# One PSUM tile of eight banks in place of four tiles of two, in a linear-attention and SwiGLU kernel

## The chip, the cores and the metric

The program runs on one core of a Trainium2 chip. The metric is device time in microseconds (us) of one execution. Three runs of the kernel before gave 236.96, 237.26 and 239.74 us; the median is 237.26 us.

## The reference, cut to what matters

Four batches of eight heads, 768 time steps, 48 features per head. `r`, `k`, `v` and `w` have the shape (4, 8, 768, 48). Step by step a 48 x 48 state per head decays and takes in the outer product of `k` and `v`:

```
y[t]  = r[t] @ (state + (u * k[t]) outer v[t])
state = w[t][:, None] * state + k[t] outer v[t]
```

The eight heads of a time step, side by side, are one row `x` of 384 values (3072 rows in all). Each row then goes through an RMS norm and a gated feed-forward layer of width 1536:

```
xn  = x / sqrt(mean(x*x) + 1e-6) * rms_g
out = (silu(xn @ w_gate) * (xn @ w_val)) @ w_out
```

## The kernel before, in words

The recurrence is cut into 6 chunks of 128 time steps (index m), and each chunk is done for the 4 batches (index j). Within a chunk the recurrence is written as matrix products: `cs` multiplies the logarithms of the decays by two triangular masks to get running sums, `exp` takes their exponential in place in PSUM, `rk` scales r and k by it, `tr` (or the DMA `trd`) turns them, `q` multiplies r by k, `qm` masks the product, `y` multiplies it by v and adds the part of the state, `st`, `sn1` and `sn` make the next state. Then come `xa` (adds the `u` term), `sq`, `rs`, `xn` (the norm), `xt` and `xe` (or the DMA `xd`; they turn the rows), and the feed-forward layer in twelve pieces per chunk: `gv` (gate or value product, 24 per chunk, each of twelve matmuls of 128 columns or of fewer and wider ones), `si` (ScalarE: silu of the gate product, PSUM to SBUF), `hm` (VectorE: value product in PSUM times that), `o` (output product in three parts of four matmuls) and `oo` (copy out of PSUM, then a DMA `od`). `warm` is a matmul of a mask with itself into bank 0; nothing reads what it writes. There are 60 of them.

The order of the work is written out by hand in the string `PLAN` (line 94): one word per step, for instance `si.5.0.11@0`, with the step's name, its indices, the slot of the ring that it writes (`@0`), and an engine where there is a choice (`/A` ScalarE, `/V` VectorE, `/G` GpSimd). For the steps that write PSUM (`dk cs tr q y xt st warm gv o`) the number behind `@` is the PSUM bank, 0 to 7; the reader of a product uses the bank that its writer was given. `cs` and `q` take two adjacent banks and always start at an even one. The steps are emitted in this order (line 537), each engine runs its own in this order, and the schedule is not changed by the framework. The kernel contains no semaphores of its own: the framework works out, from the tiles that each instruction reads or writes, which instruction has to wait for which, and adds the waits.

PSUM has 8 banks of 512 fp32 values per partition. The kernel before declares four tiles of two banks each (line 206), so banks 0 and 1 are tile `ps0`, 2 and 3 `ps1`, 4 and 5 `ps2`, 6 and 7 `ps3`. The profile prints all of them as `ps`. Two helpers hand out views: `b1` one bank, `b2` a whole tile. Every PSUM access of the kernel goes through one of them. Of the plan's words, 714 touch PSUM.

Four places of the plan that the prediction uses (lines 135, 189 to 193, cut):

```
... cs.2.1@6 sn1.2.0 warm.44 st.2.2@3 exp.2.1 sn.2.0 ...
... gv.5.0.5.g@6 gv.5.0.11.g@5 si.5.0.5@1 ...
... hm.5.0.10 gv.5.0.5.v@4 hm.5.0.3 oo.4.1@2/A o.4.0.2
si.5.0.11@0 od.4.1 hm.5.0.5 o.5.0.0@2 ... o.5.1.0@6 ...
... o.5.3.0@7 ... o.5.1.2 od.5.0 o.5.3.2 oo.5.1@0/V od.5.1
oo.5.3@1/A od.5.3
```

The product for `sn.2.0` and `sn1.2.0` was put in bank 1 (`st.2.0@1`), and `hm.5.0.3` reads bank 7 (`gv.5.0.3.v@7`).

Of the kernel before, what the change touches and what calls it, by code (L numbers as in the profile page):

```python
# [9 lines left out]
FP32 = mybir.dt.float32  # L10
# [186 lines left out]
class Env:  # L197


    def __init__(self, ctx, tc, args):  # L200
        self.slot = {}
        self.nc = nc = tc.nc
        self.r, self.k, self.v, self.w, u, self.wgate, self.wval, self.wout, g, self.out = args
        const = ctx.enter_context(tc.tile_pool(name="const", bufs=1))
        ps = ctx.enter_context(tc.tile_pool(name="ps", bufs=1, space=bass.MemoryType.PSUM))
        self.banks = [ps.tile([128, 2, 512], FP32, name=f"ps{i}") for i in range(4)]

        self.u, self.g = u, g

        def ring(name, shape, dt):  # L210
            return const.tile([128, RINGS[name]] + shape, dt, name=name)

        self.in_w = const.tile([128, 2, SB, H, D], FP32, name="in_w")
        self.in_rk = const.tile([128, 2, SB, 2, H, D], FP32, name="in_rk")
        self.in_v = const.tile([128, 2, SB, H, D], FP32, name="in_v")
        self.lw = ring("lw", [SB, H, PD], BF16)
        self.rkA = ring("rkA", [2, H, PD], BF16)
        self.rkT = ring("rkT", [2 * NP, 128], BF16)
        self.qts = ring("qts", [2, NP, 128], BF16)
        self.vb = ring("vb", [SB, H, D], BF16)  # L220
        self.ruk = ring("ruk", [H, D], FP32)
        self.ydr = ring("ydr", [H, D], FP32)
        self.xb = ring("xb", [DM], BF16)
        self.xnr = ring("xnr", [DM], BF16)
        self.xnt = ring("xnt", [KC, TS], BF16)
        self.ht = ring("ht", [FC, TS], BF16)
        self.sg = ring("sg", [TS], BF16)
        self.obr = ring("obr", [DM], FP32)
        self.u_bc = const.tile([128, H, D], FP32, name="u_bc")
        self.st = const.tile([128, 2, SB, NP, 2 * D], BF16, name="st")  # L230
        self.wg = const.tile([128, KC, DF], BF16, name="wg")
        self.wv = const.tile([128, KC, DF], BF16, name="wv")
        self.wo = const.tile([128, FC, DM], BF16, name="wo")
        self.junk = const.tile([128, DM], BF16, name="junk")
        WS = DF // NWG
        n_ht = FC * TS // (2 * KC * WS)
        self.n_ht = n_ht
        self.stage_x = const.tile([128, NSTAGE - n_ht, KC, WS], FP32, name="stage_x") if NSTAGE > n_ht else None

        self.ident = const.tile([128, 128], BF16, name="ident")  # L240
        self.mask_lt = const.tile([128, 128], BF16, name="mask_lt")
        self.mask_nle = const.tile([128, 128], BF16, name="mask_nle")
        self.wcr = ring("wcr", [SB, NP], FP32)
        self.diag = const.tile([128, NSB * SB, H, 1], FP32, name="diag")
        self.rstd = const.tile([128, NSB * SB, 2], FP32, name="rstd")
        self.g_col = const.tile([128, KC], FP32, name="g_col")
        self.ones = const.tile([128, 1], BF16, name="ones")
        self.mhalf = const.tile([128, 1], FP32, name="mhalf")
        lwf = self.lw.rearrange("p a b h d -> p (a b h) d")
        nc.vector.memset(lwf[:, :, D:PD], 0.0)  # L250
        for t, op, fill in ((self.mask_lt, ALU.is_ge, 1.0), (self.mask_nle, ALU.is_gt, -1.0)):
            nc.gpsimd.memset(t, 0.0)
            nc.gpsimd.affine_select(out=t, in_=t, compare_op=op, fill=fill, base=0, pattern=[[-1, 128]],  # L253
                                    channel_multiplier=1)
        nc.vector.memset(self.ones, 1.0)
        nc.vector.memset(self.mhalf, -0.5)
        nc.vector.memset(self.rkA.rearrange("p a b h d -> p (a b h) d")[:, :, D:PD], 0.0)
        make_identity(nc, self.ident)
        nc.vector.memset(self.st, 0.0)
# [11 lines left out]
        getattr(self, fn)(*args, *([ENGINES[eng]] if eng else []))  # L271

    def b2(self, key):
        return self.banks[self.slot[key] // 2]

    def b1(self, key):
        i = self.slot[key]
        return self.banks[i // 2][:, i % 2]

    def pair(self, t, q):  # L280
        return t[:, 2 * q:2 * q + 2, :].rearrange("p a b -> p (a b)")
# [287 lines left out]
```

## Time and profile before

| what | value |
|---|---|
| time of the profiled execution | 236.92 us |
| its span, first to last instruction on the core | 234.7 us |
| median of three runs | 237.26 us |
| TensorE (PE) busy | 206.8 us, 88% of the span |
| VectorE (DVE) busy | 163.4 us, 70% |
| ScalarE (ACT) busy | 123.3 us, 53% |
| GpSimd (POOL) busy | 99.5 us, 42% |
| granted TensorE clock, mean over the span | 0.985 of full speed |

How to read it: an engine is busy while at least one of its instructions is under way, so the shares of engines that work side by side add up to more than the span. A matmul is counted from its start to the modelled arrival of its last result. The granted clock is 1.0 at 2.4 GHz and 0.5 at 1.2 GHz. In the views by time, a line merges neighbouring instructions of one engine, line and shape; the time in brackets is how long the engine had been idle before, with the instruction that ended that idle time.

### The profile page before, as it was taken

To read this page: it belongs to the slowest core of one execution; us is meant where nothing else is said; L and a number is where in the kernel's file an instruction comes from. 1 tells how busy PE (TensorE), PEld (TensorE's weight loads), DVE (VectorE), ACT (ScalarE), POOL (GpSimd) and SP (SyncE) were. 2 spreads that over 40 slices of the span, in tenths; PEclk is the share of its full clock that TensorE was granted. 3 is DMA by queue.
4 is the path that set the end of the run, shared out by engine and by line. 5 is a ranking of instruction groups with operands and counts; after the bars stand their busy time and mean duration, and the time that the engine had idled before them with its cause. 6 is when DMAs were issued, how large, how long until landed. Compare 5 with 4: busy or idle time off the path is not lost.

```text
span 234.7 us, 4827 instructions
## 1 busy us (share of the span) xinstructions
PE 206.8 (88%) x1833; PEld 124.0 (53%) x1844; DVE 163.4 (70%) x275; ACT 123.3 (53%) x213; POOL 99.5 (42%) x143
## 2 busy tenths in 40 slices
PE   7756878999989999998798999899999889999993
PEld 2323567975667657755354455454454434544451
DVE  4668969457998879896977868888675846325331
ACT  3338786474475673678364376554774514135300
POOL 2478876913365662767214698852100200100000
PEclk9997799999999999999999999999999999999999
DMA  7999899997989989986999989931047030200013
GB/s 145 192 237 288 244 309 220 203 220 177 199 183 214 182 172 193 202 172 159 203 190 198 195 154 207 230 98 31 18 90 162 17 87 18 62 22 3 13 63 126
DMA packets 133799, 35.77 MB, mean 152 GB/s; under 512 B 124432, under 2 KB 133776, under 8 KB 133776
## 3 DMA queue, kind: packets, MB, share of 16 engines
q1 hardware_dynamic: 132192, 34.29, 67.1%
q0 software_dynamic: 1584, 1.18, 3.7%
q8 instruction: 14, 0.23, 0.4%
q14 instruction: 9, 0.07, 0.1%
HBM read 26.15 MB, written 4.72 MB: 132 GB/s over the span
## 4 chain that ended last, share of the span: by engine, by line
PE 56%; DVE 20%; ACT 8%; issue 5%; SPq 5%; DMA 4%; DVEq 0%; ACTq 0%
PE ps L493 28%; PE ps L509 18%; DVE ht L501 7%; ACT sg L497 5%; SPq L288 4%; DVE st L423 3%; DVE rkA L364 2%; DVE qts L392 2%; PE ps L356 2%; PE ps L480 2%; DMA in_rk<-in_k_dram 2%; DVE xb L449 2%; DVE xnr L462 1%; PE ps L405 1%; DMA xnt<-xnr 1%
## 5 line engine op out<-in xcount | busy, mean ns | idle before, releaser
L497 ACT ACTIVATE sg<-ps 128x512 bf16<-128x512 f32 x72 | 42.3, 596 | 56.5 <-PE ps L493 32.2
L501 DVE TENSOR_TENSOR ht<-ps,sg 128x512 bf16<-128x512 f32 x72 | 48.0, 687 | 26.3 <-ACT sg L497 17.6
L493 PE MATMUL ps<-xnt,wg 128*128 128x128 bf16 (+2 forms) x356 | 56.3, 296 | 5.4 <-ACT sg L497 1.1
L493 PE MATMUL ps<-xnt,wv 128*128 128x128 bf16 (+2 forms) x353 | 54.4, 292 | 3.1 <-ACT sg L497 1.5
L509 PE MATMUL ps<-wo,ht 128*128 128x384 bf16 x288 | 52.0, 326 | 2.2 <-DVE ht L501 1.1
L493 PEld LDWEIGHTS <-wg 128*128 128x128 bf16 x360 | 28.7, 99 | 21.7 <-issue 6.7
L493 PEld LDWEIGHTS <-wv 128*128 128x128 bf16 x360 | 28.6, 97 | 20.3 <-issue 4.0
L509 PEld LDWEIGHTS <-ht 128*128 128x128 bf16 x288 | 27.5, 98 | 22.5 <-issue 3.8
L445 POOL TENSOR_TENSOR ydr<-in_v,diag 128x384 f32<-128x384 f32 x24 | 20.7, 866 | 28.0 <-DVE diag L440 23.1
L433 POOL TENSOR_TENSOR ruk<-in_rk 128x384 f32<-128x384 f32 x24 | 23.9, 997 | 16.3 <-DMA in_rk<-in_k_dram 10.1
L364 DVE TENSOR_TENSOR rkA<-in_rk,ps 128x768 bf16<-128x768 f32 x24 | 22.4, 950 | 11.8 <-ACT ps L361 10.2
L392 DVE TENSOR_TENSOR qts<-ps,mask_lt 128x1024 bf16<-128x1024 f32 x24 | 29.0, 1219 | 1.9 <-PE ps L389 1.6
L458 POOL TENSOR_SCALAR rstd<-rstd 128x1 f32<-128x1 f32 x24 | 4.6, 190 | 48.4 <-ACT junk L453 47.7
L437 POOL TENSOR_TENSOR ruk<-ruk,u_bc 128x384 f32<-128x384 f32 x24 | 24.0, 1000 | 2.5 <-DMA u_bc<-in_u_dram 1.2
L361 ACT ACTIVATE ps<-ps 128x768 f32<-128x768 f32 x24 | 18.7, 795 | 10.5 <-PE ps L356 10.2
L480 PE MATMUL ps<-mask_lt 128*128 128x512 bf16 x60 | 20.3, 439 | 2.9 <-POOL mask_lt L253 1.4
L423 DVE TENSOR_TENSOR st<-ps,wcr 48x192 bf16<-48x192 f32 x40 | 13.8, 353 | 6.6 <-PE ps L493 2.7
L453 ACT ACTIVATE junk<-xb 128x384 bf16<-128x384 bf16 x24 | 12.5, 519 | 9.8 <-DVE xb L449 9.8
L449 DVE TENSOR_TENSOR xb<-ps,ydr 128x384 bf16<-128x384 f32 x24 | 13.2, 552 | 5.5 <-PE ps L405 3.3
L331 DVE COPY obr<-ps 128x384 f32<-128x384 f32 x14 | 7.8, 556 | 11.9 <-PE ps L509 10.7
L322 ACT ACT_TABLE_LOAD x12 | 15.4, 1283 | 0.9 <-PEq L553 0.7
L459 POOL TENSOR_TENSOR rstd<-rstd,mhalf 128x1 f32<-128x1 f32 x24 | 14.0, 581 | 2.0
(58 smaller groups left out, 201.1 us busy)
## 6 DMA issues: line engine op xcount, KB each, us to landing
in_w<-in_w_dram SPq DMA_DIRECT2D x24, 192.0 KB, 4.2
in_v<-in_v_dram SPq DMA_DIRECT2D x24, 192.0 KB, 3.7
in_rk<-in_r_dram SPq DMA_DIRECT2D x24, 192.0 KB, 3.8
in_rk<-in_k_dram SPq DMA_DIRECT2D x24, 192.0 KB, 3.8
out_dram<-obr SPq DMA_DIRECT2D x24, 192.0 KB, 2.1
ht<-in_moe_w_gate_dram SPq DMA_DIRECT2D x6, 384.0 KB, 5.1
stage_x<-in_moe_w_val_dram SPq DMA_DIRECT2D x4, 384.0 KB, 6.1
wo<-in_moe_w_out_dram POOLq DMA_DIRECT2D x3, 384.0 KB, 5.8
```

The source lines that it names most:

```text
L361: self.nc.scalar.activation(out=ps, in_=ps, func=AF.Exp)
L364: self.nc.vector.tensor_tensor(out=self.rkA[:, self.slot["rkA", m, j], :, :, 0:D], in0=self.in_rk[:, self.slot["in_rk", m], j], in1=self.b ...
L392: self.nc.vector.tensor_tensor(out=self.qts[:, self.slot["qts", m, j]].rearrange("p a q t -> p (a q) t"), in0=self.b2(("qb", m, j)).rearra ...
L423: self.nc.vector.tensor_tensor(out=new[p, :, c], in0=ps[p, :, c], in1=wc[p, :].to_broadcast([D, NP, D]), op=ALU.mult)
L433: self.nc.gpsimd.tensor_tensor(out=self.ruk[:, self.slot["ruk", m, j]], in0=rk[:, 0], in1=rk[:, 1], op=ALU.mult)
L437: self.nc.gpsimd.tensor_tensor(out=t, in0=t, in1=self.u_bc, op=ALU.mult)
L445: self.nc.gpsimd.tensor_tensor(out=self.ydr[:, self.slot["ydr", m, j]], in0=self.in_v[:, self.slot["in_v", m], j], in1=self.diag[:, m * SB ...
L480: self.nc.tensor.matmul(self.b1(("warmb",)), lhsT=self.mask_lt, rhs=bc_mid(self.mask_lt, 4), start=True, stop=True)
L493: self.nc.tensor.matmul(ps[:, a * n:(a + 1) * n], lhsT=w[:, c, f * 128:(f + 1) * 128], rhs=x[:, c], start=(a == 0 and c == 0), stop=(a == ...
L497: self.nc.scalar.activation(out=self.sg[:, self.slot["sg", m, g, i]], in_=self.b1(("gvb", m, g, i, "g")), func=AF.Silu)
L501: self.nc.vector.tensor_tensor(out=self.ht[:, self.slot["ht", m], fs[0]:fs[-1] + 1, t0:t0 + n], in0=self.b1(("gvb", m, g, i, "v")).rearran ...
L509: self.nc.tensor.matmul(ps, lhsT=self.ht[:, self.slot["ht", m], f, j * L:(j + 1) * L], rhs=self.wo[:, f, :], start=(f == 0), stop=(f == FC ...
```

## The change

All of PSUM is declared as one tile of eight banks. `b1` and `b2` return views of the same banks as before (`b2` is called with even numbers only). No step, slot, shape or order changes.

```diff
-        self.banks = [ps.tile([128, 2, 512], FP32, name=f"ps{i}") for i in range(4)]
+        self.banks = ps.tile([128, 8, 512], FP32, name="ps")
...
     def b2(self, key):
-        return self.banks[self.slot[key] // 2]
+        i = self.slot[key]
+        return self.banks[:, i:i + 2]
 
     def b1(self, key):
-        i = self.slot[key]
-        return self.banks[i // 2][:, i % 2]
+        return self.banks[:, self.slot[key]]
```

## Rows read from the trace of the kernel before

**Rows 1.** The page: span, and busy time of each engine with its share.

```profile
span 234.7 us, 4827 instructions
PE 206.8 (88%) x1833; PEld 124.0 (53%) x1844; DVE 163.4 (70%) x275; ACT 123.3 (53%) x213; POOL 99.5 (42%) x143
```

**Rows 2.** The page: shares of the chain that ended last, by engine.

```profile
PE 56%; DVE 20%; ACT 8%; issue 5%; SPq 5%; DMA 4%; DVEq 0%; ACTq 0%
```

**Rows 3.** By time, chunk 2: start us, us, engine, line, operation [idle before, releaser].

```profile
85.19 0.35 DVE L423 TENSOR_TENSOR st<-ps,wcr 48x192 bf16<-48x192 f32 x1
85.45 0.80 ACT L361 ACTIVATE ps<-ps 128x768 f32<-128x768 f32 x1
85.60 0.38 PE L480 MATMUL ps<-mask_lt 128*128 128x512 bf16 x1 [0.19 <-DVE st L423]
...
86.01 0.36 DVE L423 TENSOR_TENSOR st<-ps,wcr 48x192 bf16<-48x192 f32 x1 [0.47 <-PE ps L480]
```

**Rows 4.** Waits over the whole span: who for whom, us in all, times, longest.

```profile
DVE st L423 <- PE ps L480: 1.1, 3, 0.5
PE ps L480 <- DVE st L423: 0.6, 2, 0.5
```

**Rows 5.** By time, the last chunk's feed-forward layer: same columns.

```profile
220.10 1.29 DVE L501 TENSOR_TENSOR ht<-ps,sg 128x512 bf16<-128x512 f32 x2 [0.53 <-PE ps L493]
...
221.23 0.81 PE L493 MATMUL ps<-xnt,wv 128*128 128x512 bf16 x3
221.43 0.48 ACT L335 COPY obr<-ps 128x384 f32<-128x384 f32 x1 [0.90 <-PE ps L509]
...
222.08 0.60 ACT L497 ACTIVATE sg<-ps 128x512 bf16<-128x512 f32 x1 [0.17 <-PE ps L493]
222.71 0.69 DVE L501 TENSOR_TENSOR ht<-ps,sg 128x512 bf16<-128x512 f32 x1 [1.32 <-ACT sg L497]
```

**Rows 6.** By time, the last two copies out of PSUM.

```profile
225.78 4.87 PE L509 MATMUL ps<-wo,ht 128*128 128x384 bf16 x28
...
230.69 0.56 DVE L331 COPY obr<-ps 128x384 f32<-128x384 f32 x1 [1.39 <-PE ps L509]
231.28 0.48 ACT L335 COPY obr<-ps 128x384 f32<-128x384 f32 x1 [8.61 <-DVE obr L331]
```

**Rows 7.** Matmuls into PSUM: duration ns min/median/max, first and last start us.

```profile
L493 PE MATMUL ps<-xnt,wg x356: 216/273/390, 24.2 to 219.0; 128*128 128x128 bf16 x72, 128*128 128x512 bf16 x70, 128*128 128x256 bf16 x36
L480 PE MATMUL ps<-mask_lt x60: 376/379/634, 1.4 to 109.7; 128*128 128x512 bf16 x60
L356 PE MATMUL ps<-lw,mask_lt x24: 322/326/528, 5.2 to 173.6; 128*128 128x384 bf16 x24
```

**Rows 8.** Busy time over the whole span of instructions that touch PSUM.

```profile
core 0: us, PE busy (x) DVE busy (x) ACT busy (x), PEclk, DMA share, GB/s
0.00:234.70 234.70, 206.84 (x1833) 134.50 (x205) 72.91 (x120) 0.99 0.71 152
```

**Rows 9.** By time, dense matmuls of the feed-forward layer.

```profile
45.95 2.84 PE L493 MATMUL ps<-xnt,wv 128*128 128x128 bf16 x47
```

**Rows 10.** By time, from a narrower stretch: the silu that ends just before.

```profile
45.31 0.60 ACT L497 ACTIVATE sg<-ps 128x512 bf16<-128x512 f32 x1 [0.82 <-DVE ht L501]
```

**Rows 11.** Stretches: us, busy PE, PEld, DVE, ACT, POOL, granted clock, DMA share, GB/s.

```profile
13.30:20.10 6.80, 3.84 (x57) 2.49 (x58) 5.65 (x10) 3.56 (x8) 5.63 (x8) 1.00 1.05 236
20.10:27.00 6.90, 5.66 (x43) 3.33 (x42) 6.09 (x12) 5.99 (x13) 6.29 (x8) 0.51 1.02 309
27.00:34.00 7.00, 5.12 (x81) 4.03 (x80) 5.50 (x13) 5.57 (x12) 4.99 (x7) 1.00 0.94 270
```

## The prediction

> **What bounds the kernel now.** The page comes first: TensorE is busy 88% of the 234.7 us span, VectorE 70%, ScalarE 53% [rows 1], so the three engines work side by side most of the time. The chain that ended last is 56% PE, 20% DVE and 8% ACT [rows 2]: TensorE is the bound, with short turns through the others. All of PSUM's traffic is on these three. What the change can touch is who may be in PSUM at the same time as whom, so the views by time were read next, with the plan beside them, for pairs of instructions on neighbouring banks.
>
> Chunk 2 shows it best [rows 3]. `sn1.2.0` and `sn.2.0` read bank 1; between them the plan has `warm.44`, which writes bank 0 and whose result nobody reads. The warm-up nevertheless starts only when the first VectorE half has ended (0.19 us idle, released by it), and the second half starts at 86.01, 0.03 us after the warm-up's end at 85.98 (0.47 us idle, released by it). There is no data between them; they share the tile of banks 0 and 1. Meanwhile `exp.2.1` in banks 6 and 7 runs on ScalarE from 85.45 to 86.25 beside both. Such waits of state halves on warm-ups, and the other way round, occur three and two times [rows 4].
>
> Two readers do the same to each other [rows 5]. `gv.5.0.5.v` is written into bank 4 until 222.04; at 222.08 `si.5.0.11` starts, though its bank 5 had been written by an earlier step, and `hm.5.0.5`, which needs bank 4, starts only at 222.71, when that silu of bank 5 has ended. Across tiles there is overlap: the copy out of bank 3 (221.43 to 221.91) runs inside the product into bank 4, and `hm.5.0.3` on bank 7, the second of the merged pair that ends at 221.39, beside its start. At the end `oo.5.3` on bank 7 waits for the copy of bank 6 to end at 231.25 and starts at 231.28, though the product into its own bank was done by 230.65 [rows 6]. So the unit of waiting is the tile, not the bank: any two engines in one tile take turns in the order of the plan, reader and reader too.
>
> **The change, part by part.** The arithmetic of the views changes nothing: banks, shapes, steps and DMAs stay the same. The bound is the waits. If the tile is the unit, all 714 PSUM steps of the plan take turns. Counted in the plan's order, they form 561 turns (248 of PE, 195 of DVE, 118 of ACT), with 560 handovers. The sum along this single chain, at full TensorE clock:
>
> - Start: the first matmul is at 1.35 us [rows 7]: **1.4**.
> - TensorE: 206.8 us of busy time [rows 8] at least. A 128-column matmul lasts 0.216 us [rows 7] but in a dense stretch starts every (2.84 - 0.22)/46 = 0.057 us [rows 9], so at the end of a turn about 0.16 us of draining is bare. Much of that is hidden under the next matmul now; if none of it were counted yet, 248 x 0.16 = 40 us come on top, 247. Neither end is nearer by any row; I take the middle, **227**.
> - VectorE and ScalarE on PSUM: 134.5 + 72.9 [rows 8] = **207**. Today they lie beside TensorE; that cover is what goes.
> - Handovers: PE to a reader 0.04 us (222.04 to 222.08), ACT to DVE 0.03 (222.68 to 222.71) [rows 5], ACT to PE about 0.04 to 0.05 (45.91 to 45.95) [rows 9, 10], taken as 0.05 for DVE to PE too. 248 x 0.04 + 247 x 0.05 + 65 x 0.03 = **24**.
> - Work outside PSUM that gets into a turn. Behind a waiting `hm` in VectorE's queue stand `bs` and `xn`, behind a waiting `si` in ScalarE's the squares and table loads; GpSimd's `rs` and SP's transposes wait for those, and the next `hm` or `q` for them. In all VectorE has 163.4 - 134.5 = 28.9 us and ScalarE 123.3 - 72.9 = 50.4 us of it [rows 1, 8]: between 0 and 79. Most runs while another engine has its turn; I take a quarter, **20**. Loads on SP's queue go out later, but they are spread over more time.
> - End: from the last copy's end, 231.28 + 0.48 = 231.76 [rows 6], to 234.7, **2.9**, and the profiled execution's 236.92 less its span, **2.2**.
>
> Sum: 485 us, against 236.92 for the same execution before (0.3 under the median of 237.26). The gain that would have to be set against it is nothing: no instruction goes.
>
> **The clock** is the large unknown. TensorE would be busy 227 of 485 us, 47%. In the trace the granted clock was 1.00 from 13.3 to 20.1 us while PE was busy 3.84 of 6.80 us (56%), then 0.51 in the next 6.9 us while it was busy 82%, then 1.00 again [rows 11]. So a stretch busier than my average was followed by 1.2 GHz, and I expect it to fall. At 1.2 GHz matmuls take 528 ns for 326 and 634 for 379 [rows 7]; the issuing part of TensorE's time, 227 - 40 = 187 us, doubles, and with the clock low throughout the sum is 485 + 187 = 672 us, with PE busy 414 of 672 (62%). Whether that share brings the clock back no row says: it lies between the 56% ahead of the fall and the 82% ahead of the rise. Output products come in dense blocks [rows 6], which speaks for coming back now and then; attention steps, with short matmuls between long VectorE steps, for staying low. I take 45% of the time at 2.4 GHz and 55% at 1.2: 1/(0.45/485 + 0.55/672) = **573 us**.
>
> The Trainium skill, "TensorE: Matmul & The Clock Gate", Part 1, says that the throttled state is the default and that activity releases it, while an idle stretch brings it back. By that rule alone, as this chain leaves TensorE no long idle stretch, the clock would stay up and the time be 485; the fall at 20 us, after 6.8 us in which PE was busy 56%, speaks against relying on it.
>
> **The rivals.**
> 1. *Clock up throughout, 485 us.* For it: feed-forward pieces give TensorE two products in a row. Against: the row of 13.3 to 20.1 us. Chance 0.15 (taken as under 520).
> 2. *Clock down nearly throughout, 672 us.* For it: the share of 62% at that clock is below the only share after which it rose. Against: dense output blocks. Chance 0.20 (over 625).
> 3. *The change doesn't do what it says: nothing moves, 237 us.* The trace can't tell "one tile" from "one pair of banks, 4 KB": in the kernel before both are the same. If the framework's unit were the pair, the waits would be the same to the letter. For it: every false wait that I read is inside a pair. Against: a pair of banks is no unit that anything in this program suggests except its tiles. Chance 0.12. The Trainium skill's "PSUM — Partial Sum Buffer", section "Summary: rules for kernel authors", asks only for a different bank (or quadrant) when PSUM is read while a matmul runs. By that rule no turn-taking across banks is needed, and the time would stay at 237. The trace shows waits that are coarser than this rule, at 86.01 and 222.71 us.
> 4. *Faster: in the larger tile the banks are told apart.* Then the neighbours' waits would go. Its place is TensorE's idle time, 234.7 - 206.8 = 27.9 us [rows 1], of which only waits like the two in [rows 3] would vanish; the state halves and warm-ups cost 1.1 + 0.6 us [rows 4]. With a fifth of the idle time gone it is about 231 us. It decides if a view's banks, not its tile, set the waits. Against: two banks of one tile are not told apart now. Chance 0.03.
>
> **How the numbers follow.** Forecast 573 us, chance 0.50 (520 to 625); rivals 0.15, 0.20, 0.12, 0.03. The range reaches over rivals 1 and 2 with the small terms' bounds: 485 less 20 for TensorE's lower end, 465; 672 with about a third more of the work outside PSUM, 28, gives 700. That leaves out rivals 3 and 4 and the far ends of the bounds, together just under 0.2. Slower by over 2%: 0.50 + 0.15 + 0.20 = 0.85; within 2% (about what the runs, 236.96 to 239.74, can tell from no change): 0.12; faster: 0.03.
>
> **What the new profile would show.** That turns are taken: TensorE's share near 50 to 65%, DVE's near 30%, ACT's near 20%, with a sum of 105 to 125% instead of 211%; PSUM steps of different banks, such as `hm.5.0.3` and `gv.5.0.5.v`, no longer overlapping anywhere; silu waiting for VectorE and the reverse as the longest waits, and the chain of waits passing through DVE with a third of the span. The clock: slices of PEclk at 5 among those at 9. The size is wrong if the busy time of PSUM instructions isn't the chain, for instance with more than 40 us of issue or DMA in it. The whole is wrong if `exp` in banks 6 and 7 still runs beside a warm-up in bank 0: then the unit isn't the tile, and the time is within 2%, or less.

## The result, and the profile after

The changed kernel takes **227.34 us** (225.63 to 228.77, four runs) against 238.5 for the kernel before in the same comparison (236.96 to 242.66, four runs): a ratio of **0.955, interval 0.944 to 0.966**. The ratio is taken over the fast runs and so leaves out the one of 242.66 us; their means are 238.0 and 227.3 us, 10.7 apart. The forecast of 573 us was wrong by more than a factor of two, and on the wrong side. What happened is rival 4, which had a chance of 0.03 and a price of 231 us. The profiled execution is the slowest of the four, 228.77 us with a span of 226.6, and that of the kernel before was its fastest; the differences between the two traces are therefore a little small.

The page of the changed kernel, span and busy times, the clock's slices and the chain's shares; it answers to [rows 1, 2]:

```profile
span 226.6 us, 4842 instructions
...
PE 204.6 (90%) x1844; PEld 124.5 (55%) x1844; DVE 162.4 (72%) x275; ACT 122.6 (54%) x213; POOL 99.2 (44%) x143
...
PEclk9995889999999999999999999889999999999999
...
PE 53%; DMA 14%; DVE 12%; POOL 8%; SPq 7%; issue 4%; ACT 1%; DVEq 0%; POOLq 0%; ACTq 0%
```

The busy times are nearly those of before: the sum over PE, DVE and ACT is 216% of the span, where 211% stood and 105 to 125% was forecast. The span is 8.1 us shorter. TensorE's idle time went from 234.7 - 206.8 = 27.9 us to 22.0, its busy time fell by 2.2. In the chain, DVE and ACT fell from 28% to 13%, and what came in their place is transfers and GpSimd: 22% where 4% stood.

PSUM instructions alone, over the span [rows 8]: time, busy PE, DVE and ACT, granted clock, DMA share, GB/s:

```profile
0.00:226.60 226.60, 204.58 (x1844) 133.30 (x205) 72.71 (x120) 0.97 0.74 158
```

The plan, and with it the work of every engine, is the same (both programs have 1844 matmuls; the trace of before lacks the records of 11); what differs is when a step may start. By time, the place in chunk 2 of [rows 3] (start us, us, engine, line, operation, idle before and its releaser):

```profile
79.89 0.72 DVE L423 TENSOR_TENSOR st<-ps,wcr 48x192 bf16<-48x192 f32 x2
79.94 0.38 PE L480 MATMUL ps<-mask_lt 128*128 128x512 bf16 x1
...
80.14 0.80 ACT L361 ACTIVATE ps<-ps 128x768 f32<-128x768 f32 x1 [0.40 <-PE ps L356]
```

The two state halves on bank 1 stand in one row (79.89 to 80.61) without a gap, and the warm-up in bank 0 runs beside them, 79.94 to 80.32. The `exp` on banks 6 and 7 starts at 80.14, beside the warm-up too. That is the sign which the prediction named as showing it wrong in whole. The Trainium skill, "PSUM — Partial Sum Buffer", section "Summary: rules for kernel authors", asks only for a different bank or quadrant when PSUM is read while a matmul runs; this row of the changed kernel agrees, while the row of the kernel before showed a wait that the rule does not ask for.

The place of [rows 5], the last chunk's feed-forward layer:

```profile
213.40 1.99 DVE L501 TENSOR_TENSOR ht<-ps,sg 128x512 bf16<-128x512 f32 x3 [0.54 <-PE ps L493]
...
213.84 0.81 PE L493 MATMUL ps<-xnt,wv 128*128 128x512 bf16 x3
...
214.42 0.60 ACT L497 ACTIVATE sg<-ps 128x512 bf16<-128x512 f32 x1
```

`si.5.0.11` reads bank 5 from 214.42 while `gv.5.0.5.v` still writes bank 4 (until 214.65), and `hm.5.0.5` on bank 4, the third in its row, runs from about 214.7, beside the rest of that silu: VectorE has three `hm` in one row of 1.99 us, where the third waited before until the silu had ended.

The end, [rows 6]:

```profile
222.49 0.56 DVE L331 COPY obr<-ps 128x384 f32<-128x384 f32 x1 [0.74 <-PE ps L509]
223.14 0.48 ACT L335 COPY obr<-ps 128x384 f32<-128x384 f32 x1 [8.12 <-PE ps L509]
```

The last copy is now released by the product into its own bank, not by the other copy. Of the two waits in [rows 4], neither is left among the waits. Silu's wait for `hm` (ACT `sg` for DVE `ht`) fell from 13.6 to 8.4 us over the span, that of `hm` for products from 8.3 to 5.1.

**Where the gain is made, and where a part is given back.** The same steps in both traces, starts in us:

| step | before | after | difference |
|---|---|---|---|
| `gv.0.3.2.g` | 43.69 | 41.66 | -2.0 |
| `tr.1.3` | 67.18 | 63.30 | -3.9 |
| `warm.45` | 86.47 | 80.81 | -5.7 |
| `gv.2.0.1.g` | 125.28 | 121.30 | -4.0 |
| `gv.3.0.2.v` | 156.47 | 154.00 | -2.5 |
| `gv.4.0.6.g` | 194.82 | 188.84 | -6.0 |
| `o.5.3.0` | 227.08 | 219.69 | -7.4 |

By 87 us the change is 5.7 us ahead; from there to 157 us it loses 3.2 of them and then gains again. Stretches of the kernel before (time, busy PE, PEld, DVE, ACT, POOL, clock, DMA share, GB/s):

```profile
40.00:87.00 47.00, 43.83 (x507) 32.58 (x505) 35.25 (x61) 28.17 (x47) 25.46 (x32) 1.00 1.00 194
87.00:150.00 63.00, 56.29 (x507) 33.12 (x509) 51.53 (x87) 36.98 (x60) 37.85 (x51) 1.00 0.97 188
```

and of the changed kernel:

```profile
40.00:87.00 47.00, 46.65 (x547) 34.64 (x545) 38.29 (x68) 29.51 (x47) 27.05 (x34) 1.00 1.05 210
87.00:150.00 63.00, 53.43 (x468) 30.30 (x464) 47.02 (x79) 35.45 (x58) 36.80 (x49) 0.97 0.96 186
```

Up to 87 us TensorE is left idle 0.35 us of 47, where it was 3.2. From 87 to 150 it is idle 9.6 of 63, where it was 6.7. Waits of the changed kernel in that stretch (us in all, times, longest) name the transfers:

```profile
POOL ruk L433 <- DMA in_rk<-in_k_dram: 9.5, 2, 6.4
ACT vb L335 <- DMA in_v<-in_v_dram: 7.9, 3, 3.9
...
PE ps L389 <- DMA rkT<-rkA: 4.3, 4, 1.8
```

In the same stretch of the kernel before, the first of these is 5.9 us and the second 1.1. It looks as if work that comes earlier meets loads and transposes that don't; the experiments test the loads.

A part of what is given back is the clock. In the kernel before it stayed at 2.4 GHz from 27 us to the end of the span. In the changed kernel it fell once more, at 146.0 us, after 5 us in which TensorE was busy 2.37 us, and came back at 149.4:

```profile
141.00:146.00 5.00, 2.37 (x25) 1.01 (x24) 3.61 (x7) 1.36 (x3) 4.75 (x6) 1.00 1.08 220
146.00:149.50 3.50, 3.50 (x10) 1.27 (x9) 1.09 (x2) 1.79 (x3) 1.52 (x2) 0.51 1.01 219
```

An estimate: 3.5 us at half speed do 1.75 us of full-speed work less, so the clock may hold about half of the 3.2 us.

### The profile page after: what moved, and what is told of

Read it like the earlier page. It is cut to its first block, busy times and chain, and to the rows that moved or that the text cites. A ratio compares the mean times of both kernels' runs of the same rounds, so it can differ in the third digit from the quotient of the medians.

```text
span 226.6 us, 4842 instructions
## 1 busy us (share of the span) xinstructions
PE 204.6 (90%) x1844; PEld 124.5 (55%) x1844; DVE 162.4 (72%) x275; ACT 122.6 (54%) x213; POOL 99.2 (44%) x143
## 4 chain that ended last, share of the span: by engine, by line
PE 53%; DMA 14%; DVE 12%; POOL 8%; SPq 7%; issue 4%; ACT 1%; DVEq 0%; POOLq 0%; ACTq 0%
PE ps L493 30%; PE ps L509 13%; SPq L288 6%; DMA in_rk<-in_r_dram 5%; DMA in_w<-in_w_dram 3%; POOL ruk L433 3%; DMA rkT<-rkA 3%; PE ps L389 2%; POOL ruk L437 2%; DVE xb L449 2%; DVE st L423 2%; DMA in_rk<-in_k_dram 2%; DVE xnr L462 2%; PE ps L480 1%; DMA xnt<-xnr 1%
## 5 line engine op out<-in xcount | busy, mean ns | idle before, releaser
L493 PE MATMUL ps<-xnt,wg 128*128 128x128 bf16 (+2 forms) x360 | 57.1, 301 | 1.6 <-DMA xnt<-xnr 1.6
L493 PE MATMUL ps<-xnt,wv 128*128 128x128 bf16 (+2 forms) x360 | 55.1, 296 | 0.0
L509 PE MATMUL ps<-wo,ht 128*128 128x384 bf16 x288 | 51.1, 326 | 0.0
L440 DVE TENSOR_REDUCE diag<-ruk 128x8 f32<-128x384 f32 x24 | 13.0, 546 | 4.7 <-POOL ruk L437 4.5
L389 PE MATMUL ps<-rkT 48*128 48x128 bf16 x192 | 10.0, 226 | 6.8 <-DMA rkT<-rkA 4.3
L423 DVE TENSOR_TENSOR st<-ps,wcr 48x192 bf16<-48x192 f32 x40 | 13.7, 352 | 2.0 <-PE ps L416 1.6
```

What stands on the lines that cost most here:

```text
L423: self.nc.vector.tensor_tensor(out=new[p, :, c], in0=ps[p, :, c], in1=wc[p, :].to_broadcast([D, NP, D]), op=ALU.mult)
L493: self.nc.tensor.matmul(ps[:, a * n:(a + 1) * n], lhsT=w[:, c, f * 128:(f + 1) * 128], rhs=x[:, c], start=(a == 0 and c == 0), stop=(a == ...
L509: self.nc.tensor.matmul(ps, lhsT=self.ht[:, self.slot["ht", m], f, j * L:(j + 1) * L], rhs=self.wo[:, f, :], start=(f == 0), stop=(f == FC ...
```

## Experiments

### Are the waits the whole difference, and which of them?

Four kernels keep the one tile of eight banks and put the waits between neighbours in a pair of banks back by hand, all or one kind: `UNIT = 2`; in a kind, P is TensorE and R a reader of PSUM, and the first letter waits for the second.

```diff
     for step in PLAN.split():
+        env.touched = []; n = len(tc.nc.cur_bb.bb.instructions)
         env.step(step)
+        new = tc.nc.cur_bb.bb.instructions[n:]
+        for u in {b // UNIT for b in env.touched}:
+            ...  # for the last instruction `name` of each other engine in u, if its kind is in KINDS
+                tc.add_manual_dep(new[0], name, info, reason="unit of banks")
```

**All three kinds.** 

> One tile of eight banks, with the waits between the two banks of a pair put back by hand: before a PSUM step, its first instruction waits for the last step of each other engine in banks 0-1, 2-3, 4-5 or 6-7. Theory A (the gain is these waits and nothing else): back to the kernel before, 235 to 240 us, ratio 0.99 to 1.01. Theory B (the gain comes from the tile itself, its addressing or fewer wait instructions, and the neighbours' waits were harmless): near the changed kernel, 226 to 229 us, ratio 0.955.

Measured: 241.82 us, ratio 1.013 (1.005 to 1.020).

**TensorE waits for a reader of the neighbour bank** (`KINDS = ['PR']`). 

> Of the waits of e1 only those of TensorE for a reader (VectorE or ScalarE) in the neighbouring bank. Theory A1 (what costs is TensorE held up by a reader of a bank it doesn't write): most of the 11 us come back, 234 to 238 us. Theory A2 (what costs is readers held up by TensorE): 227 to 230 us.

Measured: 234.38 us, 0.981 (0.973 to 0.988).

**A reader waits for TensorE's step in the neighbour bank** (`['RP']`). 

> Of the waits of e1 only those of VectorE and ScalarE for TensorE writing the neighbouring bank. Theory A1: 227 to 231 us. Theory A2: 234 to 238 us, since a late reader also frees its bank late.

Measured: 233.36 us, 0.981 (0.974 to 0.987).

**Reader and reader** (`['RR']`). 

> Of the waits of e1 only those of VectorE for ScalarE and the reverse, each reading one bank of a pair. Both theories: small, 226 to 230 us; over 232 us would say that readers held up by each other are what cost.

Measured: 229.53 us, 0.962 (0.957 to 0.967).

With all waits put back the gain is gone, although the tile stays as changed: the waits are the difference, not the tile. It is a little more than gone: 241.82 us lies above the 235 to 240 us of Theory A, and the interval lies above 1. The waits by hand are stricter than those of before, since they stand ahead of a step's first instruction, and in TensorE's steps that is the weight load. In the kernel before, the weights of the warm-up in [rows 3] were loaded at 85.09 us and only its matmul, at 85.60, waited for the state half:

```profile
85.09 0.10 PEld L480 LDWEIGHTS <-mask_lt 128*128 128x128 bf16 x1
```

With all waits put back by hand, the load waits too:

```profile
86.88 0.10 PEld L482 LDWEIGHTS <-mask_lt 128*128 128x128 bf16 x1 [0.57 <-DVE st L425]
86.89 0.39 PE L482 MATMUL ps<-mask_lt 128*128 128x512 bf16 x1 [0.19 <-DVE st L425]
```

So what TensorE's waits cost here is an upper end. Neither kind alone holds the gain. Waits of TensorE and waits of the readers give back 0.981 - 0.955 = 0.026 each; the reader pairs' 0.007 lies inside the intervals and isn't clear of noise. Together they make 0.058, which is what all three do at once (1.013 - 0.955). The expectation that one kind would carry most of it falls. The stretch 40 to 87 us of the four, in the order above:

```profile
40.00:87.00 47.00, 43.82 (x514) 32.40 (x512) 35.37 (x61) 28.21 (x48) 26.09 (x32) 1.00 0.99 190
```

```profile
40.00:87.00 47.00, 45.41 (x518) 33.28 (x518) 37.22 (x64) 29.60 (x48) 26.66 (x33) 1.00 1.03 206
```

```profile
40.00:87.00 47.00, 44.17 (x537) 33.73 (x537) 38.05 (x65) 28.43 (x48) 26.23 (x34) 1.00 0.95 184
```

```profile
40.00:87.00 47.00, 46.19 (x534) 34.16 (x532) 37.37 (x67) 29.95 (x49) 27.66 (x35) 1.00 1.04 207
```

TensorE's busy time goes back to that of before (43.83) with all kinds, to between the two with the first two, and stays nearly up with the last.

### Is it one tile, or the eight banks in one tile?

The kernel before with two tiles of four banks, so that a tile is larger but not the whole of PSUM:

```diff
-        self.banks = [ps.tile([128, 2, 512], FP32, name=f"ps{i}") for i in range(4)]
+        self.banks = [ps.tile([128, 4, 512], FP32, name=f"ps{i}") for i in range(2)]
...
-        return self.banks[self.slot[key] // 2]
+        i = self.slot[key]
+        return self.banks[i // 4][:, i % 4:i % 4 + 2]
```

> PSUM as two tiles of four banks each. Theory C (the waits go by whole tiles unless one tile holds all of PSUM): every engine takes turns with the others in each half of PSUM, so slower than the kernel before by much, 280 to 420 us. Theory D (a tile of two banks is a special case, and in any larger tile the banks are told apart): 226 to 229 us. Theory E (the unit is a pair of banks in tiles of two and four): 237 us.

Measured: 314.56 us, **1.318** (1.307 to 1.329).

```profile
span 311.2 us, 4832 instructions
...
PE 229.0 (74%) x1833; PEld 130.2 (42%) x1844; DVE 167.0 (54%) x275; ACT 123.9 (40%) x213; POOL 99.0 (32%) x143
...
PE 48%; DVE 27%; ACT 12%; issue 5%; SPq 4%; DMA 2%; POOL 1%; DVEq 0%; ACTq 0%
```

In tiles of four, the four banks take turns: DVE and ACT hold 39% of the chain (13% in the changed kernel), as the prediction had it for one tile of eight. By time, the place in chunk 2 of [rows 3]:

```profile
115.02 0.80 ACT L362 ACTIVATE ps<-ps 128x768 f32<-128x768 f32 x1 [0.57 <-PE ps L357]
115.26 0.33 PE L417 MATMUL ps<-vb,rkA 128*128 128x96 bf16 x4
115.63 0.36 DVE L424 TENSOR_TENSOR st<-ps,wcr 48x192 bf16<-48x192 f32 x1 [0.80 <-PE ps L417]
115.86 0.32 PE L357 MATMUL ps<-lw,mask_lt 128*128 128x384 bf16 x1 [0.27 <-ACT ps L362]
```

`sn.2.0` on bank 1 now waits for `st.2.2` in bank 3 to end (115.59), and `cs.2.3` in banks 4 and 5 for `exp.2.1` in banks 6 and 7 (115.82). In the kernel before, `st.2.2` ran beside `sn.2.0` (86.01 in [rows 3]) and `cs.2.3` started while `exp.2.1` ran (until 86.25):

```profile
85.97 0.33 PE L416 MATMUL ps<-vb,rkA 128*128 128x96 bf16 x4
86.14 0.33 PE L356 MATMUL ps<-lw,mask_lt 128*128 128x384 bf16 x1
```

So "the unit is the tile" holds for two and for four banks and fails for eight; the pair of banks (rival 3) is no unit, since with it this kernel would be as fast as before.

### Was the prediction's sum right for what it assumed?

The changed kernel with every PSUM step made to wait for the last of every other engine, `UNIT = 8` with all three kinds in the edit above: the turn-taking that was forecast.

> One tile of eight banks, with the waits put in by hand that the prediction took for granted: before a PSUM step its first instruction waits for the last PSUM step of each other engine, whatever the bank. This measures the prediction's sum by itself. If the sum and its clock are right: 573 us, with 485 as its value at full clock and 672 at half. If work on TensorE, VectorE and ScalarE overlaps more than by turns, under 450.

Measured: 625.8 us, **2.622** (2.601 to 2.644), within the 465 to 700 that was given.

```profile
span 621.5 us, 4872 instructions
...
PE 366.5 (59%) x1833; PEld 155.8 (25%) x1844; DVE 167.6 (27%) x275; ACT 124.5 (20%) x213; POOL 98.3 (16%) x143
...
PEclk9999999755576555565656765555565566568588
```

```profile
0.00:621.50 621.50, 366.48 (x1833) 140.64 (x205) 74.52 (x120) 0.66 0.27 58
```

The turns themselves, by time, at the end:

```profile
592.18 0.81 PE L495 MATMUL ps<-xnt,wg 128*128 128x512 bf16 x3
593.10 0.69 DVE L503 TENSOR_TENSOR ht<-ps,sg 128x512 bf16<-128x512 f32 x1 [7.27 <-PE ps L495]
...
593.85 0.82 PE L495 MATMUL ps<-xnt,wv 128*128 128x512 bf16 x3 [0.86 <-DVE ht L503]
594.71 0.60 ACT L499 ACTIVATE sg<-ps 128x512 bf16<-128x512 f32 x1 [3.24 <-PE ps L495]
...
595.36 0.82 PE L511 MATMUL ps<-wo,ht 128*128 128x384 bf16 x4 [0.69 <-ACT sg L499]
```

One engine ends, the next begins within 0.04 to 0.11 us. The three engines' times in PSUM add up to 366.5 + 140.6 + 74.5 = 581.6 us; with the 24 us of handovers of the prediction 606 of the 621.5 are accounted for. The clock was lower than taken: its mean of 0.665 means half speed for 67% of the time, where 55% was taken; the prediction's own formula with that share, 1/(0.33/485 + 0.67/672), gives 596. The other run of this kernel had a mean of 0.585, half speed for 83% of the time, and took 627.88 us against 623.71; the formula gives 35 us between these two shares, so its step from clock to time is rough.

### What gives a part back from 87 to 150 us?

Is it TensorE itself? First the changed kernel without the warm-ups `warm.30` to `warm.59`, which are left out of the plan and whose results nobody reads:

```diff
-sn1.1.0 ld.1.3.v warm.30 qm.1.0@2 warm.31 exp.1.2 warm.32 warm.33 ld.1.3.k ...
+sn1.1.0 ld.1.3.v qm.1.0@2 exp.1.2 ld.1.3.k ...
```

> The changed kernel without the warm-up matmuls 30 to 59. In its trace 29 of these 30 are followed by the next matmul without a gap, each 0.216 us of TensorE's issue: 6.3 us. Theory F (TensorE is the bound there now that the waits are gone): 2 to 6 us less than the changed kernel, 222 to 225 us. Theory G (loads and DMA transposes set the pace from 87 to 150 us): they give it back, 226 to 228 us; if the clock falls more often without them, 229 or more.

Measured: 228.73 us, 0.958 (0.953 to 0.963). Then the changed kernel with two products put ahead of `q.4.3` and `q.4.1`, which wait for transfers:

```diff
-sn.4.0 q.4.3@4 ruk1.5.1@0 bs.5.3 q.4.1@6 oo.2.2@0/A gv.3.0.4.g@3 qm.4.3@1 od.2.1 ruk2.5.1 gv.3.0.6.v@0 od.2.2
+gv.3.0.4.g@3 gv.3.0.6.v@0 sn.4.0 q.4.3@4 ruk1.5.1@0 bs.5.3 q.4.1@6 oo.2.2@0/A qm.4.3@1 od.2.1 ruk2.5.1 od.2.2
```

> The changed kernel with two products of the feed-forward layer (gv.3.0.4.g, gv.3.0.6.v) moved ahead of q.4.3, for which TensorE waits 1.78 us on a DMA transpose at 141.9 us before the clock falls at 146.0. Theory F: the wait is filled and the clock stays up, 2 to 3 us less than the changed kernel, 224 to 226 us. Theory G: the products were not late, the time stays at 227 to 228.

Measured: 229.55 us, 0.962 (0.956 to 0.968). Neither gains. The stretch from 87 us in the two:

```profile
87.00:150.00 63.00, 55.09 (x475) 31.25 (x478) 49.20 (x81) 35.35 (x58) 36.76 (x49) 0.95 0.99 193
```

```profile
87.00:150.00 63.00, 54.30 (x484) 31.98 (x485) 48.80 (x81) 35.22 (x57) 37.73 (x50) 0.97 0.99 188
```

Work taken off TensorE, or moved into its gap, leaves the end where it was, which speaks against TensorE as the bound here. In the first of them the clock was also lower in this stretch (0.95 against 0.97, by estimate 1.3 us of 63), and that is less than the 6.3 us taken off.

Then the loads. Both kernels with half of the heads loaded for chunks 2 and later (4 of 8; the engines' work stays):

```diff
-        self.nc.sync.dma_start(out=t, in_=getattr(self, w)[j, :, m * L:(m + 1) * L, :]...)
+        n = H if m < 2 else H // 2
+        self.nc.sync.dma_start(out=t[:, 0:n], in_=getattr(self, w)[j, 0:n, m * L:(m + 1) * L, :]...)
```

The changed kernel: 

> The changed kernel with half of r, k, v and w loaded in chunks 2 to 5 (heads 0 to 3; the other heads keep the values of an earlier chunk), so it leaves out half of those transfers and no instruction of an engine. Theory G (from 87 to 150 us loads and transposes set the pace, and there the changed kernel gave gain back: TensorE idle 9.6 of 63 us): 218 to 222 us. Theory F (loads aren't what held it): 226 to 228 us.

Measured: **217.61 us**, 0.918 (0.910 to 0.925). The kernel before: 

> The kernel before with the same half of the transfers left out. Theory G: it was held by its own waits there more than by loads, so it gains less than the changed kernel does, 233 to 237 us, and the distance between the two grows from 11 us to 14 or more. Theory F: 237 to 239 us and the distance stays.

Measured: 237.18 us, 0.9985 (0.994 to 1.003). The stretch from 87 us, changed and before:

```profile
87.00:150.00 63.00, 62.62 (x576) 36.31 (x574) 58.82 (x100) 41.81 (x73) 41.65 (x59) 1.00 0.67 136
```

```profile
87.00:150.00 63.00, 57.30 (x513) 33.46 (x512) 52.39 (x88) 37.61 (x61) 37.92 (x52) 1.00 0.72 140
```

The half of the loads costs the kernel before nothing that can be measured and the changed one 0.955 - 0.918 = 0.037, some 9 us: without it TensorE is idle only 0.4 of 63 us, and the clock stays up (1.00 against 0.97). The distance between the two kernels grows from 10.7 to 19.5 us, as Theory G had it, though the time of the kernel before is that of Theory F. That is what the change is worth with half of the loads.

Is it the total of the transfers? The transposes of `rkA` by DMA were replaced by TensorE's, in chunks 3 and 4 and in chunks 2 to 4, for instance:

```diff
-trd.3.0@0
+tr.3.0@3 ... tre.3.0@0/A
```

Chunks 3 and 4: 

> The changed kernel with the eight DMA transposes of r and k in chunks 3 and 4 (trd) replaced by the way of chunks 0 and 1: eight matmul transposes on TensorE (tr, into a free bank) and a copy by ScalarE (tre). It takes transfers off the stretch of 87 to 150 us and adds 8 x 0.6 us of TensorE and 8 x 1.0 us of ScalarE there. Theory G (transfers set the pace there and TensorE has 9.6 us to spare): 222 to 226 us, faster than both kernels. If the added TensorE and ScalarE work or the waits for it eat the gain: 227 to 230 us.

Measured: 228.66 us, 0.963 (0.958 to 0.968). Chunks 2 to 4: 

> The same for chunk 2 too (twelve transposes). Theory G: 221 to 225 us, as long as TensorE, 99% busy from 40 to 87 us, isn't made the bound there, which would give back up to 4 x 0.45 us. If the added work eats it: 228 to 231 us.

Measured: 229.49 us, 0.965 (0.961 to 0.969). The stretch in the first of them:

```profile
87.00:150.00 63.00, 56.36 (x540) 34.20 (x538) 48.42 (x80) 42.68 (x66) 36.89 (x49) 1.00 0.79 158
```

The DMA engines' share fell from 0.96 to 0.79 and nothing was gained. In the second of them it fell to 0.67, as with half of the loads:

```profile
87.00:150.00 63.00, 58.46 (x570) 36.15 (x571) 49.51 (x80) 45.45 (x69) 35.93 (x49) 1.00 0.67 138
```

GpSimd's wait for the load of k, 9.5 us in the changed kernel, is down to 1.1 there, and TensorE waits for the copies that were added:

```profile
PE ps L491 <- ACT rkT L333: 3.9, 6, 0.8
POOL ruk L431 <- DMA in_rk<-in_k_dram: 1.1, 1, 1.1
```

TensorE's busy time rose by 5.0 us of the 63 (53.43 to 58.46) and ScalarE's by 10.0. So waits for transfers went and added work came in their place, the second branch of both expectations; these two runs can't tell what the transposes cost. What it is about the loads (when they are issued on SP's queue, how long they take, when their buffers come free) is **not settled** by these runs.

## Why the prediction was wrong

**The step that failed** is the carrying over from two banks to eight: "So the unit of waiting is the tile, not the bank", and on it "If the tile is the unit, all 714 PSUM steps take turns". What was read in [rows 3, 5, 6] was right: steps on different banks of one tile did wait, and putting such waits back (1.013) undoes the whole gain. But every tile of the kernel before has two banks. No row could tell "a tile" from "a tile of this size", and the prediction said as much only of the pair (rival 3).

What sets the waits was looked up afterwards in the programs as built, which is a reading of their waits and no measurement. Of the more than 700 waits across engines in the kernel before, some 150 await a step in the other bank of the same tile; in the changed kernel none does; with two tiles of four some 300 do, over all four banks. In small programs, where VectorE fills one bank and ScalarE reads another of the same tile, the second step is made to wait from 5 partitions on in a tile of two banks, from 3 on in a tile of four, and never in a tile of eight, up to all 128 partitions. It looks as if a view's reach is counted at the tile's row length (4, 8 and 16 KB in one partition) and, once partitions times row length passes 16 KB, the step counts as touching all of the tile; only where the row is the whole 16 KB do the banks stay apart. That rule is read off these cases and not shown beyond them. On the chip this has been run at three sizes: two banks (238.5 us), four (314.56) and eight (227.34), and the order agrees.

**The sum** was right for its premise: the turns run by hand take 625.8 us, and TensorE stops 253 times in that trace, where 248 turns were counted. Its readers' 207 us measured 215 (140.6 + 74.5), and what is left of the span 40 against 48 (24 + 20 + 1.4 + 2.9). Two terms were too low. One is the clock, 55% of the time at half speed against 67% in the profiled run (573 to 596 by the formula); the fall itself was foreseen from [rows 11]. The other is TensorE's own time: with 67% of the time at half speed, 0.594 of the work is done there, and the sum has TensorE busy 40 + 187 x 1.594 = 338 us (an estimate). It was busy 366.5, so the middle between 207 and 247 was too low. The Trainium skill, "TensorE: Matmul & The Clock Gate", Part 1, has an idle stretch bring the throttled state back; by that rule alone, as the prediction took it, the time would have been 485. The measured 625.8 does not agree with it: before the first fall no idle stretch of TensorE was longer than 1.95 us.

**Rival 3** (nothing changes, 0.12) falls with the result and with tiles of four. **Rival 4** (faster, 0.03) has the right mechanism, "if a view's banks, not its tile, set the waits", and nearly the price, 231 us from a fifth of TensorE's idle time. A fifth is 5.6 us, and 5.9 went; that is luck, since no row gave the fifth, and with half of the loads the change is worth 19.5 us. The remaining 2.2 us of the span are less busy time of TensorE, although its clock was lower (0.97 against 0.99 in the PSUM rows). An estimate from the two traces: TensorE stops 70 times before and 27 times after, and 43 ends of turns fewer, at the prediction's 0.16 us of bare draining, are 6.9 us; 6.8 us more at half speed (13.7 against 6.8) take back up to 3.4. Against the rival stood only that "two banks of one tile are not told apart now", true of tiles of two banks. With no row on larger tiles, that argument did not bear a chance as low as 0.03, nor the forecast's turns 0.85.

**The price of single waits** was read too low: the three and two waits of [rows 4] sum to 1.7 us, but two kinds of such waits cost up to 0.026 each, some 6 us. Many of them stand elsewhere, as [rows 5, 6] show, between products and `hm`, silu and output copies, where the waits view files them under lines that also have true waits.

**What the prediction did not have** is the second bound: that the gain would be cut by transfers: 10.7 us are left of the 19.5 that half of the loads allows. [rows 2] gave DMA 4% of the chain, and the share of the DMA engines near 1.00 in [rows 11] was not weighed, as the forecast left the loads more time.

## What to carry to other kernels

A wait between steps with no data between them belongs to the way the program reckons what a step touches, not to the chip; how it reckons for a tile of another shape can't be read from tiles of one shape, so the waits of the new program must be looked at before one side is given most of the chance. Here a PSUM tile of all eight banks keeps the banks apart, tiles of two make neighbours take turns (4.5% of the time), and tiles of four cost 32%. A gain on the bounding engine can be cut by a second bound: leaving out half of the loads in both kernels shows how much it was here (10.7 us against 19.5).

## What was not expected of the hardware

In the kernel with all turns taken by hand, TensorE's clock stayed at 2.4 GHz for 116 us and then fell to 1.2 without a long idle stretch before. Three stretches, up to the first return:

```profile
0.00:100.00 100.00, 58.62 (x447) 37.51 (x448) 31.37 (x59) 27.87 (x54) 32.18 (x48) 1.00 0.57 125
100.00:116.40 16.40, 8.11 (x63) 4.24 (x60) 5.61 (x8) 4.83 (x7) 2.77 (x3) 1.00 0.04 13
116.40:174.50 58.10, 33.88 (x204) 16.96 (x205) 16.09 (x29) 10.23 (x17) 7.05 (x10) 0.50 0.47 95
```

TensorE was busy 59% of the first 100 us and 49% of the 16.4 us before the fall. The longest idle stretch there was 1.88 us; two of 1.88 and 1.95 us, at 51 and 55 us, had not been followed by a fall. After the fall it was busy 58% again, but at half speed, with 3.5 matmuls in a us in place of 4.5, so equal shares at the two levels are not equal work. Once down, the clock came back only for short times (the slices of PEclk above). What made it fall at 116 us and not earlier stays open.

And the DMA engines' share was no measure of whether transfers hold the kernel: at 0.67 from 87 to 150 us half of the loads gave 9 us, and twelve transposes moved to TensorE gave nothing, with the work that they added.
